# An attention, routing and feed-forward kernel: GpSimd takes over the splitting of k and q, exponentials go ahead of transposes, and weight splits in the assignment move to VectorE

## The chip, the cores and the metric

The kernel runs on one core of one Trainium2 chip. The metric is the device time of one execution in microseconds; runs are compared by their median. PE is TensorE, DVE is VectorE, ACT is ScalarE, POOL is GpSimd, SP is the engine that issues most transfers.

## The reference

Three parts follow each other, all in float32 on the outside.

```python
# 1. attention within hash buckets; q, k, v: [2, 8, 768, 64], proj: [64, 6]
q_bucket, k_bucket = six sign bits of q @ proj and of k @ proj
scores = where(q_bucket == k_bucket, q @ k.T / 8, -1e9)
attn = exp(scores - rowmax);  attn /= attn.sum() + 1e-9
x = (attn @ v), heads side by side            # [1536, 512]
# 2. eight experts, each takes at most 192 of the 1536 tokens
logits = x @ w_gate                           # [1536, 8]
# greedy: largest logit first; a token goes to one expert, a full expert takes no more
out[tokens of e] = relu(x[tokens of e] @ w1[e]) @ w2[e]      # w1[e]: [512, 1024]
# 3. RMS norm, then a gated feed-forward layer, 512 -> 1536 -> 512
xn = x / sqrt(mean(x*x) + 1e-6) * rms_g
y = (silu(xn @ w_gate2) * (xn @ w_val)) @ w_out
```

The three weights of part 3 arrive as 64-bit floats.

## The kernel before

**Numbers in two parts.** A product that needs float32 precision is done in the matmul type float32r, with each operand split into a rounded high part and the low remainder (`nh`, `nl` for k and q; `wh`, `wl` for the experts' weights). Splitting is two instructions: a rounding copy, and a subtract.

**Attention.** Heads are taken in pairs: 2 batches x 4 pairs, 8 pairs in all. A pair has six tiles of 128 queries, and each of its two heads is one iteration `u`, so 12 iterations for a pair and 96 in all. The program is written out in order by hand (no scheduler); each engine works through its own list. In iteration u stand: six transposes of the probabilities of u into two PSUM tiles and their evacuation (`transp`), the exponential of u+1 (`expo`), the scores of u+2 with their row minimum (`scores`; scores carry a minus sign), half of the product with v (`pv`), and every second iteration the combination of two heads (`comb`, which also multiplies by the experts' gate weights, 64 + 8 columns for a head) and its scaling by the inverse row sums (`rinv`, `comb_v`). PSUM tiles called `m` come from a pool of three that transposes, combination and preparation share.

**Work filled in between.** A table `fill` adds work to iterations: the preparation of the next pair and the conversion of the 64-bit weights. Preparation `prep_t` transposes half of k or q (three transposes), ACT writes the rounded `nh` from PSUM, DVE subtracts into `nl`; 4 halves for a pair, 28 in all, since the first pair is prepared by other code. `prep_d` sends `nh` and `nl` into stacked operands by transfers on SP. `prep_p` (12 products on PE, then one DVE comparison for each half) forms the hash bits; it stands four iterations after the last half of q. Then SP sends the bits (`prep_s`), and one iteration later issues the next pair's loads. A conversion `conv` comes every 2.4 iterations, 36 in all: two DVE instructions, one on ACT, then four on GpSimd one behind the other; its store (`conv_store`) stands on SP four iterations later. SP's list is in order too, so a store that waits holds everything behind it.

**Assignment.** Three rounds of `share` on DVE and PE find who gets which expert: DVE compares whole tables (`above`, into `reach`), PE counts (`reached`), DVE waits for the count. A last step (`choose_left`, `positions`) yields the row numbers; GpSimd gathers rows of x from memory, and all engines take a branch that is for a rare case (`tc.If`). Within the first two rounds stand the splits of the first expert's eight weight pieces (`split_w`): ACT rounds, GpSimd subtracts, and SP loads the next piece into the space that the subtract has released.

**Experts and feed-forward.** These fill the rest of the time, nearly all of it PE work. The change leaves their instructions as they are.

Of the kernel before, what the change touches and what calls it, by code (L numbers as in the profile page):

```python
# [43 lines left out]
def lsh_attention__moe__swiglu_kernel(ctx, tc, q, k, v, proj, m_wg, m_w1, m_w2,  # L44
# [158 lines left out]
    def split_w(i, dve_hi, pool_lo):  # L203
        raw = WR.pop(i)
        WH[i] = wth.tile([128, 1024], F32R, name="wh")
        WL[i] = wth.tile([128, 1024], F32R, name="wl")
        if dve_hi:
            nc.vector.tensor_copy(WH[i], raw)
        else:
            nc.scalar.activation(WH[i], raw, AF.Copy)  # L210
        (nc.gpsimd if pool_lo else nc.vector).tensor_tensor(WL[i], raw, WH[i], op=OP.subtract)  # L211
        if i + 8 < 8 * E:
            load_w(i + 8)

# [19 lines left out]
    def conv(n):  # L234
# [9 lines left out]
        nc.gpsimd.tensor_scalar(ha.bitcast(F32), ha.bitcast(F32), MINEXP, None, op0=OP.max)  # L244
# [9 lines left out]
    NAT, STK = {}, {}  # L254

    def prep_t(p, nm, half):
        if half == 0:
            NAT[nm, p] = (nat.tile([128, S], F32R, name="nh_" + nm),
                          nat.tile([128, S], F32R, name="nl_" + nm))
            if nm == "k":  # L260
                SG[p] = nat.tile([128, S], F32R, name="sg")
# [3 lines left out]
        for i in range(TPB // 2):  # L265
            nc.tensor.transpose(t[:, i * 128:(i + 1) * 128],
                                LD[nm, p][:, half * (TPB // 2) + i].rearrange("p h d -> p (h d)"), ident)
        if nm == "q":
            nc.scalar.activation(nh[:, cs], t[:, :HALF], AF.Copy, scale=QS)
            nc.vector.scalar_tensor_tensor(nl[:, cs], t[:, :HALF], QS, nh[:, cs], op0=OP.mult, op1=OP.subtract)  # L270
        else:
            nc.scalar.activation(nh[:, cs], t[:, :HALF], AF.Copy)
            nc.vector.tensor_tensor(nl[:, cs], t[:, :HALF], nh[:, cs], op=OP.subtract)
# [36 lines left out]
    def scores(u):  # L310
# [12 lines left out]
        for n in range(2):  # L323
# [4 lines left out]
        nc.vector.scalar_tensor_tensor(rs[:, h, 2:3], rs[:, h, 0:1], BIG / 2, rs[:, h, 0:1],  # L328
                                       op0=OP.is_lt, op1=OP.mult)
# [10 lines left out]
    def transp(u):  # L340
        pt = PR.pop(u).rearrange("p a b -> p (a b)")
        o = wk.tile([128, TPB, 128], F32, name="pt", bufs=4)
        for half in range(2):
# [4 lines left out]
            if half == 0 or u % 4 < ACT_EVAC:  # L348
                nc.scalar.activation(o[:, 3 * half:3 * half + 3, :], t, AF.Copy)  # L349
            else:  # L350
                nc.vector.tensor_copy(o[:, 3:6, :], t)
# [34 lines left out]
    def rinv(i):  # L386
        rs = RS.pop(i)
        ri = wk.tile([128, 2, 2], F32, name="ri", bufs=2)
        nc.vector.tensor_scalar(ri[:, :, 0], rs[:, :, 3], 1e-9, None, op0=OP.add)
# [3 lines left out]
    def comb_v(i):  # L393
# [292 lines left out]

    def share(r, pieces=()):
        t1 = aw.tile(SH, F32, name="t1")
# [17 lines left out]
        for i in pieces:  # L706
            split_w(i, False, True)
# [9 lines left out]
        above(1, 1)  # L717
        pf = reached(1)
# [545 lines left out]
```

## Time and profile before

| | us |
|---|---|
| three timed runs | 843.48, 842.15, 839.46; median 842.15 |
| profiled execution, its own time | 836.1 |
| its span, first to last instruction | 834.3 |
| PE / DVE / ACT / POOL busy in the span | 763.9 / 553.6 / 398.9 / 329.7 |

The span is what the trace covers; 1.8 us of the profiled execution lie around it. Busy time is an average over stages with different limits: attention runs to about 303 us, the assignment to about 354, experts and feed-forward to the end.

### The profile page before, as it was taken

How to read it: one execution, taken by the hardware profiler on the slowest of the kernel's cores; microseconds unless marked ns; L12 is line 12 of the kernel's file. 1: busy time of each engine (PE TensorE's matmuls, PEld its weight loads, DVE VectorE, ACT ScalarE, POOL GpSimd, SP SyncE). 2: the span in 40 equal slices, each digit the busy share in tenths (PEclk: the TensorE clock that was granted, in tenths of full speed). 3: DMA queues.
4: the chain of work that ended last, by engine and by line, in shares of the span. 5: the costliest groups of instructions: out<-in, count | busy, mean ns of one | idle time of the engine just before them, and what ended most of it. 6: DMA issues, size and time to landing. Idle time of an engine off the chain costs nothing.

```text
span 834.3 us, 14721 instructions
## 1 busy us (share of the span) xinstructions
PE 763.9 (92%) x5317; PEld 685.0 (82%) x5317; DVE 553.6 (66%) x1345; ACT 398.9 (48%) x863; POOL 329.7 (40%) x251
## 2 busy tenths in 40 slices
PE   7999999998999952499999998999999999999996
PEld 4787777777878842289989998999999999999996
DVE  7799899899999987558888776575432332233222
ACT  3676667676676770057767765544311221121111
POOL 3077777766777856237657662000100010001001
PEclk7999999999999995599999999999999999999999
DMA  3678879796988425137767833274200010001000
GB/s 77 170 205 243 229 234 287 210 298 189 265 216 239 156 69 165 28 95 246 228 200 228 265 119 114 76 228 126 80 23 1 30 47 0 1 1 39 1 1 38
DMA packets 95474, 114.00 MB, mean 137 GB/s; under 512 B 31404, under 2 KB 68268, under 8 KB 95396
## 3 DMA queue, kind: packets, MB, share of 16 engines
q1 hardware_dynamic: 93316, 106.71, 43.6%
q0 software_dynamic: 1920, 6.29, 2.1%
q8 instruction: 44, 0.72, 0.4%
q14 instruction: 34, 0.28, 0.1%
q10 hardware_dynamic: 160, 0.00, 0.0%
HBM read 76.83 MB, written 18.09 MB: 114 GB/s over the span
## 4 chain that ended last, share of the span: by engine, by line
PE 35%; issue 18%; DVE 2%; POOL 1%; ACT 1%; DMA 1%; SPq 0%; POOLq 0%; ACTq 0%; DVEq 0%
PE pg L1151 6%; PE pv L1151 6%; PE py L994 6%; PE po L1179 6%; PE ph L970 4%; PE py L996 3%; PE ph L972 2%; POOL out_dram L1187 1%; PE ph L948 1%; DMA fraw<-wv_d 1%; DVE wl L211 0%; PE py L1067 0%; PE px L1026 0%; DVE yn L1056 0%; DVE xl L930 0%
## 5 line engine op out<-in xcount | busy, mean ns | idle before, releaser
L1187 POOL DMA_INDIRECT out_dram<-ot,oi x12 | 11.7, 975 | 312.3 <-DVE ot L1185 310.5
L211 POOL TENSOR_TENSOR wl<-wr,wh 128x1024 fp32r<-128x1024 f32 x43 | 106.3, 2485 | 52.8 <-PE ph L948 20.3
L336 ACT ACTIVATE pr<-sc,rs 128x768 f32<-128x768 f32 x96 | 95.2, 992 | 20.2 <-DVE rs L328 16.0
L347 PE MATMUL m<-ident,pr 128*128 128x128 f32 x576 | 85.6, 282 | 13.2 <-ACT pr L336 8.3
L1160 DVE TENSOR_TENSOR a<-sg,pg 128x384 f32<-128x384 f32 x48 | 26.6, 553 | 105.6 <-ACT sg L1158 105.6
L326 DVE TENSOR_REDUCE rs<-sc 128x1 f32<-128x768 f32 x96 | 91.1, 949 | 7.9 <-PE sc L324 6.2
L244 POOL TENSOR_SCALAR ha<-ha 128x512 f32<-128x512 f32 x36 | 57.3, 1593 | 90.7 <-DVE ha L242 90.7
L347 PEld LDWEIGHTS m<-ident,pr 128*128 128x128 f32 x576 | 62.1, 140 | 30.8 <-ACT pr L336 16.3
L366 PE MATMUL xo<-pt,ld_v 128*64 128x128 f32 x1128 | 82.3, 281 | 0.0
L970 PE MATMUL ph<-xg,wh 128*128 128x384 f32 x256 | 75.3, 362 | 6.5 <-DVE ht L987 5.8
L349 ACT ACTIVATE pt<-m 128x384 f32<-128x384 f32 x120 | 56.3, 490 | 51.2 <-PE m L347 50.5
L994 PE MATMUL py<-ht,wh 128*128 128x384 f32 x256 | 77.3, 366 | 0.0
L1158 ACT ACTIVATE sg<-pg 128x384 f32<-128x384 f32 x48 | 23.5, 490 | 108.7 <-PE pg L1151 108.7
L366 PEld LDWEIGHTS xo<-pt,ld_v 128*64 128x64 f32 x1128 | 59.6, 136 | 18.6 <-issue 11.7
L1164 ACT ACTIVATE ah<-a 128x384 fp32r<-128x384 f32 x48 | 25.2, 525 | 99.8 <-DVE a L1161 99.8
L1151 PE MATMUL pg<-xh,gl 128*128 128x384 f32 x192 | 64.6, 336 | 0.0
L1151 PE MATMUL pg<-xl,gh 128*128 128x384 f32 x192 | 64.5, 336 | 0.0
L1151 PE MATMUL pg<-xh,gh 128*128 128x384 f32 x192 | 64.5, 336 | 0.0
L1151 PE MATMUL pv<-xh,vl 128*128 128x384 f32 x192 | 64.4, 335 | 0.0
L1151 PE MATMUL pv<-xl,vh 128*128 128x384 f32 x192 | 64.4, 335 | 0.0
L1151 PE MATMUL pv<-xh,vh 128*128 128x384 f32 x192 | 64.4, 335 | 0.0
L996 PE MATMUL py<-ht,wl 128*128 128x192 f32 x256 | 64.0, 254 | 0.0
(249 smaller groups left out, 1976.9 us busy)
## 6 DMA issues: line engine op xcount, KB each, us to landing
wr<-in_moe_w_dram SPq DMA_DIRECT2D x64, 512.0 KB
w<-in_moe_w_gate_dram SPq DMA_DIRECT2D x12, 512.0 KB
w<-in_moe_w_val_dram SPq DMA_DIRECT2D x12, 512.0 KB
w<-in_moe_w_out_dram SPq DMA_DIRECT2D x12, 512.0 KB
s_k<-nh_k SPq DMA_DIRECT2D x28, 192.0 KB
s_q<-nh_q SPq DMA_DIRECT2D x28, 192.0 KB
ld_k<-in_k_dram SPq DMA_DIRECT2D x16, 192.0 KB
ld_q<-in_q_dram SPq DMA_DIRECT2D x16, 192.0 KB
```

Source lines behind the costliest of these rows:

```text
L211: (nc.gpsimd if pool_lo else nc.vector).tensor_tensor(WL[i], raw, WH[i], op=OP.subtract)
L244: nc.gpsimd.tensor_scalar(ha.bitcast(F32), ha.bitcast(F32), MINEXP, None, op0=OP.max)
L326: nc.vector.tensor_reduce(rs[:, h, 0:1], ps[:, :, :HALF], axis=AX.XY, op=OP.min)
L336: nc.scalar.activation(pt, ps[:, :, :HALF], AF.Exp, scale=rs[:, h, 1:2], bias=rs[:, h, 2:3], accum_out=rs[:, h, 3:4])
L347: nc.tensor.transpose(t[:, i, :], pt[:, c * 128:(c + 1) * 128], ident)
L349: nc.scalar.activation(o[:, 3 * half:3 * half + 3, :], t, AF.Copy)
L366: nc.tensor.matmul(xo[64 * h:64 * h + 64], vt[:, h, c, :], a[h][:, c, :], start=(c == 0), stop=(c == TPB - 1))
L970: hi = lambda: nc.tensor.matmul(ph[:, :2 * CAP], wh[:, d], xg[:, d].rearrange("p a b -> p (a b)"), start=(d == 0), stop=(d == KD - 1), ski ...
L994: hi = lambda: nc.tensor.matmul(py[d][:, :2 * CAP], wh[:, ds], ht[:, f].rearrange("p a b -> p (a b)"), start=(f == 0), stop=(f == KF - 1), ...
L996: lo = lambda: nc.tensor.matmul(py[d][:, :CAP], wl[:, ds], ht[:, f, 0], start=False, stop=False, skip_group_check=True)
L1151: nc.tensor.matmul(t[:, :TJ], a[:, d, :], b_[:, d, :], start=(n == 0), stop=(n == 3 * KD - 1))
L1179: nc.tensor.matmul(PO[j][t], a[:, ts], b_, start=(f == 0 and n == 0), stop=(f == KG - 1 and n == 2))
```

## The change

Six edits in attention and one in the assignment. (1) `prep_t`: ACT copies k or q from PSUM to a new tile `raw`, and GpSimd makes `nh` and `nl` from it; DVE has no part in it any more. (2) `expo(u + 1)` stands ahead of `transp(u)`, and of the two evacuations of u the first half goes to DVE and the second to ACT (before, the other way round; one iteration in four has both on ACT). (3) One of the two small instructions behind the row minimum takes a column as pointer operand in place of a second tensor. (4) `rinv` adds 1e-9 column by column. (5) `comb_v` scales all 72 columns of a head at once into a wider `xs`; GpSimd copies the logits' columns to `lp` once for a pair, except for the last pair of a batch, and x is written with one transfer for each head. (6) The first GpSimd instruction of a conversion has two ALU operations, minimum and maximum, instead of one. (7) In the assignment ACT rounds all eight pieces first, DVE does the subtracts: two in each round of `share`, the last two behind the gathers.

```diff
-    def split_w(i, dve_hi, pool_lo):
-        raw = WR.pop(i)
+    def split_hi(i, dve):
         WH[i] = wth.tile([128, 1024], F32R, name="wh")
         WL[i] = wth.tile([128, 1024], F32R, name="wl")
...
+    def split_lo(i, pool):
+        (nc.gpsimd if pool else nc.vector).tensor_tensor(WL[i], WR.pop(i), WH[i], op=OP.subtract)
         if i + 8 < 8 * E:
             load_w(i + 8)
+
+    def split_w(i, dve_hi, pool_lo):
+        split_hi(i, dve_hi)
+        split_lo(i, pool_lo)
...
-        nc.gpsimd.tensor_scalar(ha.bitcast(F32), ha.bitcast(F32), MINEXP, None, op0=OP.max)
+        nc.gpsimd.tensor_scalar(ha.bitcast(F32), ha.bitcast(F32), 3.0e38, MINEXP, op0=OP.min, op1=OP.max)
...
+            RAW[nm, p] = nat.tile([128, S], F32, name="nr_" + nm)
...
         if nm == "q":
-            nc.scalar.activation(nh[:, cs], t[:, :HALF], AF.Copy, scale=QS)
-            nc.vector.scalar_tensor_tensor(nl[:, cs], t[:, :HALF], QS, nh[:, cs], op0=OP.mult, op1=OP.subtract)
+            nc.scalar.activation(raw[:, cs], t[:, :HALF], AF.Copy, scale=QS)
         else:
-            nc.scalar.activation(nh[:, cs], t[:, :HALF], AF.Copy)
-            nc.vector.tensor_tensor(nl[:, cs], t[:, :HALF], nh[:, cs], op=OP.subtract)
+            nc.scalar.activation(raw[:, cs], t[:, :HALF], AF.Copy)
+        nc.gpsimd.tensor_copy(nh[:, cs], raw[:, cs])
+        nc.gpsimd.tensor_tensor(nl[:, cs], raw[:, cs], nh[:, cs], op=OP.subtract)
...
-        nc.vector.scalar_tensor_tensor(rs[:, h, 2:3], rs[:, h, 0:1], BIG / 2, rs[:, h, 0:1],
-                                       op0=OP.is_lt, op1=OP.mult)
+        nc.vector.tensor_scalar(rs[:, h, 2:3], rs[:, h, 0:1], BIG / 2, rs[:, h, 0:1], op0=OP.is_lt, op1=OP.mult)
...
-            if half == 0 or u % 4 < ACT_EVAC:
+            if half == 1 or u % 4 < ACT_EVAC:
                 nc.scalar.activation(o[:, 3 * half:3 * half + 3, :], t, AF.Copy)
             else:
-                nc.vector.tensor_copy(o[:, 3:6, :], t)
+                nc.vector.tensor_copy(o[:, 0:3, :], t)
...
-        nc.vector.tensor_scalar(ri[:, :, 0], rs[:, :, 3], 1e-9, None, op0=OP.add)
+        for h in range(2):
+            nc.vector.tensor_scalar(ri[:, h, 0:1], rs[:, h, 3:4], 1e-9, None, op0=OP.add)
...
-            XS[p] = wk.tile([128, TPB, 2, D], F32, name="xs", bufs=2)
+            XS[p] = wk.tile([128, TPB, 2, W], F32, name="xs", bufs=2)
...
+        if hp == HP - 1:
+            nc.vector.tensor_tensor(lp[:, c, 2 * hp:2 * hp + 2, :], pcv[:, :, D:],
+                                    ri[:, :, 1:2].to_broadcast([128, 2, E]), op=OP.mult)
         if i < NU // 2 - 1:
-            nc.vector.tensor_tensor(XS[p][:, t], pcv[:, :, :D],
-                                    ri[:, :, 1:2].to_broadcast([128, 2, D]), op=OP.mult)
+            nc.vector.tensor_tensor(XS[p][:, t], pcv, ri[:, :, 1:2].to_broadcast([128, 2, W]), op=OP.mult)
+        if t == TPB - 1 and hp < HP - 1:
+            nc.gpsimd.tensor_copy(lp[:, b * TPB:(b + 1) * TPB, 2 * hp:2 * hp + 2, :], XS[p][:, :, :, D:])
...
     for u in range(NU + 3):
+
+        if u + 1 < NU:
+            expo(u + 1)
         if u < NU:
             transp(u)
-        if u + 1 < NU:
-            expo(u + 1)
...
     def share(r, pieces=()):
...
-        for i in pieces:
-            split_w(i, False, True)
+        piece()
         pn = reached(0)
...
         above(1, 1)
+        piece()
         pf = reached(1)
...
+    for i in range(8):
+        split_hi(i, False)
     for r in range(3):
-        share(r, (range(0, 4), range(4, 8), ())[r])
+        share(r, range(2 * r, 2 * r + 2))
...
+    for i in (6, 7):
+        split_lo(i, False)
     rv = flagged()
```

`piece()` takes the next number of `pieces` and calls `split_lo` for it on DVE.

The order of the instructions shows the moves at three places. The first is ACT in the first iterations of attention. Before, an evacuation of transposes (`pt`) stands ahead of each exponential (`pr`):

```order
L349 ACTIVATE pt_868<-m_869 128x384
L336 ACTIVATE pr_879,rs_822<-sc_823,rs_822 128x768
L371 ACTIVATE xt_898<-xo_835 128x128
L269 ACTIVATE nh_q_900<-m_902 128x384
L349 ACTIVATE pt_909<-m_910 128x384
L336 ACTIVATE pr_920,rs_822<-sc_881,rs_822 128x768
```

And in the changed kernel, at the same place:

```order
L342 ACTIVATE pr_877,rs_831<-sc_832,rs_831 128x768
L355 ACTIVATE pt_879<-m_885 128x384
L377 ACTIVATE xt_908<-xo_843 128x128
L276 ACTIVATE nr_q_912<-m_913 128x384
L342 ACTIVATE pr_921,rs_831<-sc_890,rs_831 128x768
L355 ACTIVATE pt_923<-m_929 128x384
```

The exponential has changed places with the evacuation of the iteration before it, and ACT writes `nr_q` (raw) where it wrote `nh_q`.

The second place is GpSimd in the middle of attention. Before, its list there holds nothing but conversions, four instructions each:

```order
L244 TENSOR_SCALAR ha<-ha 128x512
L245 TENSOR_TENSOR ha<-ha,eight 128x512
L246 TENSOR_TENSOR ha<-ha,lr 128x512
L247 TENSOR_TENSOR ha<-ha,sg 128x512
L244 TENSOR_SCALAR ha<-ha 128x512
```

And now, around the second half of a preparation (`nr` is raw):

```order
L249 TENSOR_SCALAR ha<-ha 128x512
L250 TENSOR_TENSOR ha<-ha,eight 128x512
L251 TENSOR_TENSOR ha<-ha,lr 128x512
L252 TENSOR_TENSOR ha<-ha,sg 128x512
L279 CAST nh_q<-nr_q 128x384
L280 TENSOR_TENSOR nl_q<-nr_q,nh_q 128x384
L414 COPY lp<-xs 128x6x16
L249 TENSOR_SCALAR ha<-ha 128x512
```

A rounding and a subtract have come in between two conversions, and once for a pair the copy of the logits' columns.

The third place is DVE in the first round of `share`. Before:

```order
L698 TENSOR_TENSOR oh<-lg,m 128x96
L670 TENSOR_TENSOR reach<-steps,kb 128x1536
L701 TENSOR_REDUCE bids<-oh 128x12
L681 TENSOR_SCALAR full_4541<-prank 128x8
L710 TENSOR_TENSOR t_4545<-oh,pcut 128x96
L712 TENSOR_REDUCE own<-t_4545 128x12
L713 SCALAR_TENSOR_TENSOR kb<-own,kv 128x12
L670 TENSOR_TENSOR reach<-steps,kb 128x1536
L716 TENSOR_SCALAR whole<-pcut 128x8
L670 TENSOR_TENSOR reach<-steps,kb 128x1536
L681 TENSOR_SCALAR full_4579<-prank 128x16
```

And now:

```order
L682 TENSOR_TENSOR reach<-steps,kb 128x1536
L721 TENSOR_REDUCE bids<-oh 128x12
L212 TENSOR_TENSOR wl<-wr,wh 128x1024
L693 TENSOR_SCALAR full_4612<-prank 128x8
L729 TENSOR_TENSOR t_4616<-oh,pcut 128x96
L731 TENSOR_REDUCE own<-t_4616 128x12
L732 SCALAR_TENSOR_TENSOR kb<-own,kv 128x12
L682 TENSOR_TENSOR reach<-steps,kb 128x1536
L735 TENSOR_SCALAR whole<-pcut 128x8
L682 TENSOR_TENSOR reach<-steps,kb 128x1536
L212 TENSOR_TENSOR wl<-wr,wh 128x1024
L693 TENSOR_SCALAR full_4653<-prank 128x16
```

A subtract (`wl`) stands ahead of each of the two instructions (`full`) that wait for PE's count.

## Rows read from the trace of the kernel before

**Rows 1.** Windows, attention: us, busy of PE, PEld, DVE, ACT, POOL, clock, DMA, GB/s.

```profile
22.00:303.00 281.00, 264.68 (x2379) 221.72 (x2378) 253.82 (x682) 192.76 (x423) 187.36 (x144) 1.00 0.78 219
```

**Rows 2.** Timeline of PE: start, duration, line, op, out<-in, [idle before <-releaser].

```profile
22.64 0.82 PE L347 MATMUL m<-ident,pr 128*128 128x128 f32 x6
...
128.96 0.82 PE L347 MATMUL m<-ident,pr 128*128 128x128 f32 x6
...
131.84 0.83 PE L347 MATMUL m<-ident,pr 128*128 128x128 f32 x6
...
146.41 0.88 PE L347 MATMUL m<-ident,pr 128*128 128x128 f32 x6 [1.17 <-ACT pr L336]
...
148.97 0.87 PE L347 MATMUL m<-ident,pr 128*128 128x128 f32 x6
...
151.28 0.44 PE L281 MATMUL m<-nh_k,pjt 128*128 128x384 f32 x1
...
153.47 0.82 PE L347 MATMUL m<-ident,pr 128*128 128x128 f32 x6
...
300.29 0.87 PE L347 MATMUL m<-ident,pr 128*128 128x128 f32 x6 [0.17 <-ACT pr L336]
```

**Rows 3.** Waits of PE, 22 to 303 us: us in total, times, longest.

```profile
PE m L347 <- ACT pr L336: 8.3, 15, 1.2
...
PE m L347 <- ACT lr L239: 0.2, 1, 0.2
```

**Rows 4.** Timeline of DVE.

```profile
144.11 1.07 DVE L328 SCALAR_TENSOR_TENSOR rs<-rs 128x1 f32<-128x1 f32 x1
```

**Rows 5.** Groups by line and form, DVE, 22 to 303 us: busy us, mean ns.

```profile
L328 DVE SCALAR_TENSOR_TENSOR rs<-rs 128x1 f32<-128x1 f32 x95 | 30.0, 316 | 0.0
...
L389 DVE TENSOR_SCALAR ri<-rs 128x2 f32<-128x2 f32 x48 | 18.7, 390 | 0.0
...
L327 DVE TENSOR_SCALAR rs<-rs 128x1 f32<-128x1 f32 x95 | 14.6, 154 | 3.3
...
L273 DVE TENSOR_TENSOR nl_k<-m,nh_k 128x384 fp32r<-128x384 f32 x14 | 7.7, 556 | 4.5 <-ACT nh_k L272 4.3
...
L401 DVE TENSOR_TENSOR lp<-m,ri 128x16 f32<-128x16 f32 x46 | 7.6, 165 | 0.0
```

**Rows 6.** Groups by line and form, POOL, same window.

```profile
L244 POOL TENSOR_SCALAR ha<-ha 128x512 f32<-128x512 f32 x36 | 57.3, 1593 | 90.7 <-DVE ha L242 90.7
L247 POOL TENSOR_TENSOR ha<-ha,sg 128x512 int32<-128x512 int32 x36 | 46.1, 1281 | 2.8
...
L245 POOL TENSOR_TENSOR ha<-ha,eight 128x512 int32<-128x512 int32 x36 | 38.1, 1058 | 3.0
```

**Rows 7.** Timeline of POOL in the assignment.

```profile
306.02 20.77 POOL L211 TENSOR_TENSOR wl<-wr,wh 128x1024 fp32r<-128x1024 f32 x8 [0.37 <-ACT wh L210]
```

**Rows 8.** Timeline of DVE in the assignment.

```profile
305.73 0.25 DVE L694 TENSOR_REDUCE kv<-kl 128x12 f32<-128x96 f32 x1
...
334.44 0.26 DVE L654 TENSOR_TENSOR drop<-kl,cut 128x96 f32<-128x96 f32 x1
...
341.83 0.17 DVE L681 TENSOR_SCALAR full<-prank 128x16 bf16<-128x16 f32 x1 [0.98 <-PE prank L678]
...
342.29 0.17 DVE L719 TENSOR_TENSOR cut<-pcut,whole 128x8 f32<-128x8 f32 x1 [0.28 <-PE pcut L684]
```

**Rows 9.** Two lines on DVE: duration ns min/median/max, first and last start us.

```profile
L211 DVE TENSOR_TENSOR wl<-wr,wh x3: 1219/1225/2574, 372.5 to 376.5; 128x1024 fp32r<-128x1024 f32 x3
...
L242 DVE TENSOR_SCALAR ha<-w x36: 406/418/1443, 41.8 to 289.4; 128x512 int32<-128x512 int32 x36
```

**Rows 10.** Timeline of DVE behind the branch.

```profile
353.83 0.17 DVE L887 TENSOR_SCALAR t<-rcs 128x12 f32<-128x12 f32 x1 [4.03 <-DVEq L877]
```

**Rows 11.** Group of splits on POOL, on the page: busy us, mean ns.

```profile
L211 POOL TENSOR_TENSOR wl<-wr,wh 128x1024 fp32r<-128x1024 f32 x43 | 106.3, 2485 | 52.8 <-PE ph L948 20.3
```

**Rows 12.** Timeline of POOL ahead of attention.

```profile
6.92 1.79 POOL L577 COPY cb<-ident 64x64 f32<-64x64 f32 x8
```

More of the change, by code (lines that the diff above doesn't have):

```diff
@@ L201, in load_w @@
         WR[i] = t
-    def split_w(i, dve_hi, pool_lo):
-        raw = WR.pop(i)
+    def split_hi(i, dve):
         WH[i] = wth.tile([128, 1024], F32R, name="wh")
         WL[i] = wth.tile([128, 1024], F32R, name="wl")
-        if dve_hi:
-            nc.vector.tensor_copy(WH[i], raw)
-        else:
-            nc.scalar.activation(WH[i], raw, AF.Copy)
-        (nc.gpsimd if pool_lo else nc.vector).tensor_tensor(WL[i], raw, WH[i], op=OP.subtract)
+        if dve:
+            nc.vector.tensor_copy(WH[i], WR[i])
+        else:
+            nc.scalar.activation(WH[i], WR[i], AF.Copy)
+    def split_lo(i, pool):
+        (nc.gpsimd if pool else nc.vector).tensor_tensor(WL[i], WR.pop(i), WH[i], op=OP.subtract)
         if i + 8 < 8 * E:
             load_w(i + 8)
+    def split_w(i, dve_hi, pool_lo):
+        split_hi(i, dve_hi)
+        split_lo(i, pool_lo)
     convs = []
@@ L252, in conv_store @@
         nc.sync.dma_start(dst[cv_at(src, i)], CV.pop(n).bitcast(F32))
-    NAT, STK = {}, {}
+    NAT, STK, RAW = {}, {}, {}
     def prep_t(p, nm, half):
@@ L267, in prep_t @@
                                 LD[nm, p][:, half * (TPB // 2) + i].rearrange("p h d -> p (h d)"), ident)
+        raw = RAW[nm, p]
         if nm == "q":
-            nc.scalar.activation(nh[:, cs], t[:, :HALF], AF.Copy, scale=QS)
-            nc.vector.scalar_tensor_tensor(nl[:, cs], t[:, :HALF], QS, nh[:, cs], op0=OP.mult, op1=OP.subtract)
-        else:
-            nc.scalar.activation(nh[:, cs], t[:, :HALF], AF.Copy)
-            nc.vector.tensor_tensor(nl[:, cs], t[:, :HALF], nh[:, cs], op=OP.subtract)
+            nc.scalar.activation(raw[:, cs], t[:, :HALF], AF.Copy, scale=QS)
+        else:
+            nc.scalar.activation(raw[:, cs], t[:, :HALF], AF.Copy)
+        nc.gpsimd.tensor_copy(nh[:, cs], raw[:, cs])
+        nc.gpsimd.tensor_tensor(nl[:, cs], raw[:, cs], nh[:, cs], op=OP.subtract)
     def prep_p(p, half):
@@ L410, in comb_v @@
             for h in range(2):
-                nc.scalar.activation(XS[p][:, t, h], pcv[:, h, :D], AF.Copy, scale=ri[:, h, 1:2])
+                nc.scalar.activation(XS[p][:, t, h], pcv[:, h], AF.Copy, scale=ri[:, h, 1:2])
         if t == TPB - 1:
-            nc.sync.dma_start(
-                x_d[b * S:(b + 1) * S, hp * 128:(hp + 1) * 128].rearrange("(c p) d -> p c d", p=128),
-                XS.pop(p).rearrange("p c h d -> p c (h d)"))
+            for h in range(2):
+                nc.sync.dma_start(
+                    x_d[b * S:(b + 1) * S, (2 * hp + h) * D:(2 * hp + h + 1) * D].rearrange("(c p) d -> p c d", p=128),
+                    XS[p][:, :, h, :D])
+            del XS[p]
     def proj_consts():
@@ L687, in share, with piece @@
     def share(r, pieces=()):
+        pieces = iter(pieces)
+        def piece():
+            for i in pieces:
+                split_lo(i, False)
+                break
         t1 = aw.tile(SH, F32, name="t1")
@@ L875, in lsh_attention__moe__swiglu_kernel @@
         gather(0, kk)
+    for i in (6, 7):
+        split_lo(i, False)
     rv = flagged()
```

2 lines of the change are left out of this document (removed).

## The prediction

> **What bounds the kernel now.** I read the stretches first, then TensorE's own order of time, then who it waits for, and last what the two vector engines spend.
>
> The window from 22 to 303 us is the attention stage. In its row [rows 1] no engine is idle for long: PE is busy 264.7 of 281 us, DVE 253.8, ACT 192.8, POOL (GpSimd) 187.4. Busy time does not say which one sets the pace, so the second step is what PE would need if nothing held it. Starts of consecutive blocks tell it [rows 2]: an even iteration u (six transposes, scores, combination, p·v) goes from 146.41 to 148.97, 2.56 us; an odd one from 148.97 to 151.28, 2.31 us; the twelve products of `prep_p` from 151.28 to 153.47, 2.19 us; and an even iteration with three transposes of `prep_t` in it from 128.96 to 131.84, 2.88 us, so those three cost 0.32. From the first transpose of u = 0 (22.64) to that of u = 95 (300.29) there are 48 even and 47 odd iterations: 48 x 2.56 + 47 x 2.31 = 231.4. Seven pairs are prepared on the way: 7 x (4 x 0.32 + 2.19) = 24.3. That makes 255.7 us, and it took 277.65. So **21.9 us** of the stage are PE held up, and no change that leaves PE's work alone can win more there.
>
> What holds it up: the waits of PE in the same window [rows 3]. The largest is for `pr`, the exponential on ACT: 8.3 us in 15 waits. There are eight rows, the first and the last stand here; those that name ACT or DVE add up to 14.0, the one that names a transfer to 1.7. The exponential is late because DVE is: the L328 that gives it scale and bias takes 1.07 us at 144.11 [rows 4], and PE then sits for 1.17 us before 146.41 [rows 2].
>
> Why a one-column instruction takes 1.07 us: the DVE table [rows 5]. L327 is one column from one SBUF operand and takes 0.154 us on average over 95. L328, one column with two SBUF operands, averages 0.316; L389, two columns, 0.390. The excess of the 1.07 us one is about the length of one GpSimd instruction [rows 6], so I read it as DVE waiting for GpSimd in some forms and not in others.
>
> The second place is the assignment. GpSimd runs eight weight splits end to end from 306.02, 20.77 us [rows 7]. Three equal rounds of `share` lie there on DVE: they start at 305.73 and the third ends at 342.29, 36.6 us; but the third, with GpSimd quiet, needs only 334.44 to 342.29, 7.85 us [rows 8].
>
> **The change part by part.**
>
> *Assignment.* No GpSimd split runs in it any more. Three rounds at 7.85 are 23.6 us: 36.6 - 23.6 = **13.0 us** saved. Six of the subtracts move to DVE, at 1.22 us each [rows 9] (fastest of the case, GpSimd not in the way). Each stands where DVE would wait for PE to count, 0.98 us before 341.83 [rows 8]; the other gap of a round is somewhat shorter. Bounds: six times 1.22 - 0.98, that is 1.4, and 7.3 with no cover. I take 2.0, since the cover is there in every round. The last two subtracts come after the gathers and ahead of the branch. Behind them on DVE stand the branch and `t3`, and for DVE's arrival PE waits. DVE today waits 4.03 us there before 353.83 [rows 10], so the two are either inside that time (0) or ahead of it (2.4). The two weight loads that they release also fall beside the gathers. I take 1.2. ACT's eight roundings ran as one run before and still do. Net: 13.0 - 2.0 - 1.2 = **9.8 us**.
>
> *Attention, DVE.* It loses 14 + 14 subtracts `nl` at 0.556 (15 us), 48 small L401 (7.6, less some for the wider joint product: 7), the waits in L328 and L389. New L328 has one tensor operand and a one-column pointer; bounds 0.154 (L327) and 0.316 (as now); I take 0.2, which is nearest to L327's form: 11 us less. L389 becomes two one-column instructions; these follow each other faster than they last, 4 us less as a floor. Together 37 of 253.8. Against it: L242 waits too (median 0.418, longest 1.443 [rows 9]) and keeps its form; it will meet a busier GpSimd, and were it to wait half a 1.3 us instruction every time, that is 36 x 0.65 = 23 us at most. DVE goes to 217 to 240 us, under PE's 256.
>
> *Attention, ACT.* exp(u+1) now stands ahead of the evacuation of u. Before, the exponential queued behind an evacuation that waits for PE, which waited for the exponential before it; that ring is cut. Work is the same: `raw` costs what `nh` did, one evacuation changes halves.
>
> *Attention, GpSimd.* This is the term that can spoil the rest. Its 187.4 us get 28 roundings and 28 subtracts of 384 columns, and six `lp` copies. Subtract: 384/1024 of 2.485 [rows 11] is 0.93. Rounding: no row has it; a copy of 64 columns takes 1.79/8 = 0.22 [rows 12], so between 0.22 and six times that, 1.34; I take 0.75, midway. With starts 0.08 apart from ends, 28 x (0.93 + 0.75 + 0.16) = 51, `lp` 2. L244 changes too: one ALU operation becomes two. Bounds: 0.22 (the copy) and twice its 1.593, 3.19. It reads one tensor of 512 and yet takes longer than L245 (1.058, one tensor and one column) and L247 (1.281, two tensors) [rows 6], so its time is no price of reading; I take L245's 1.06, the row with the same operands. GpSimd: 187.4 - 36 x 0.53 + 51 + 2 = 221 us, 240 if L244 stays as it is. Its first conversion cannot start before 42, so if PE's waits vanish there are 281 - 20 - 20 = 241 us for it. It fits, at nine tenths busy. What queues behind it: `prep_p` on PE (four iterations, about 10 us, after the last half), the stack transfers on SP, and behind them on SP the next pair's loads, for which PE waits 1.7 us already.
>
> The Trainium skill, "GPSIMD Engine Reference", section 4.1 (Engine selection), says against this move that elementwise work belongs on VectorE, GpSimd being about 2x slower for two inputs. By that page a subtract would be 2 x 0.556 = 1.1 (estimate), 5 us more in all. The row gives 0.93, so the trace is milder, and I keep it.
>
> *The rest.* x is written in 16 transfers instead of 8, in runs of 64 floats; the last is issued as attention ends and read by the gathers a whole assignment later; that distance hides it, and without it one more transfer's issue would show. Nothing behind the branch changes.
>
> Of PE's 14.0 us of waits for ACT and DVE I count **13** as won; the transfer wait and the stretches between waits stay. Sum: 836.1 (the profiled execution, whose span is 834.3) - 13 - 9.8 = 813.3. The three timed runs have a median of 842.15, 6.05 above the profiled one; I forecast for the median: 842.15 - 22.8 = **819 us**.
>
> **The rivals.**
>
> A. GpSimd takes over as the bound of attention. For it: 240 us of work in 241 if the new L244 gains nothing, and 256 if the rounding costs 1.34 as well. Then conversions lag, SP stands behind their stores, the next pair's loads come late and PE waits there. Against it: the results of conversions are needed only in the kernel's last stage, so a late one alone holds nobody. Attention wins 0 to 7, the assignment its 9.8: 825 to 832 us.
>
> B. Slower. One mechanism: two ALU operations in L244 cost two passes. GpSimd's list after 42 is then 179 + 36 t us, against 261 until 303. The gain of 9.8 is used up at t = 2.5 us; at t = 3.19 attention ends 33 us later, and the time is 842 + 33 - 10 = 865. Against it: L245's operands at 1.06.
>
> C. GpSimd's one-tensor instructions are cheap, near the copy row's end: L244 0.5, rounding 0.4. Then GpSimd has 190 us of work, never holds anybody, and attention comes close to PE's sum: 20 of the 21.9. Time: 842 - 20 - 10 = 812. The trace speaks against it with L244's 1.593 for one operation and for it with the copy row. The Trainium skill, the same section 4.1, holds that one-input work on GpSimd runs at roughly line rate, which is this case; L244 as it stands disagrees.
>
> D. The new rs form still waits for GpSimd: DVE keeps 11 us, still below PE; the forecast moves by 3 to 5 us and stays in its range.
>
> **How the numbers follow.** Forecast with D 0.58 (814 to 825), A 0.20, C 0.13, B 0.07, anything else 0.02. The range runs from C's end, with the full 21.9 and the assignment at 12 (808), to A's far end plus 3 us of unequal runs (835). A difference of 0.5%, 4.2 us, is about what a measurement of this kernel can tell. Faster by more than that: forecast, A and C, less the part of A that could vanish, 0.89; within 0.04; slower 0.07.
>
> **What the changed profile would show.** Right: DVE L328's and L389's successors at 0.15 to 0.2 throughout; waits of PE for `pr` under 3 us; a gap from the first transpose to that of u = 95 near 265 us; three rounds of `share` of about 8.5 us each; GpSimd 215 to 225 us busy in attention with L244's successor near 1.1. Wrong, by A: GpSimd without idle time and PE waiting for `nl` or for `ld_k`; by B: L244's successor over 2.5 us; for the assignment: PE's restart after the branch more than 3 us later than the last `gi`, measured against today's.

## The result and the profile after

The changed kernel takes 827.03 us (median of 828.43, 823.67, 831.96 and 825.64) against 840.81 for the kernel before on the same chip: ratio 0.987, 95% interval 0.9832 to 0.9908. By the medians it is faster by 13.8 us, where 22.8 were forecast; the ratio, which the interval belongs to, is not the quotient of the two medians (0.984) and puts the gain at 11 us (8 to 14). The profiled execution took 828.43 us, with a span of 826.3.

Attention's row in the windows of the changed kernel, 22 to 303 us, columns as in [rows 1]:

```profile
22.00:303.00 281.00, 265.54 (x2384) 223.58 (x2382) 228.85 (x676) 191.50 (x427) 199.38 (x208) 0.99 0.80 219
```

Over the whole span PE is busy 766.7 us, DVE 524.7, ACT 396.5 and POOL (GpSimd) 320.9. In attention DVE lost 25 us of work and POOL gained 12, no more. Yet PE's timeline of the changed kernel, from the transposes of u = 0 to those of u = 95, with a held-up place between them, and the restart behind the branch at its end:

```profile
22.63 0.82 PE L353 MATMUL m<-ident,pr 128*128 128x128 f32 x6
...
120.99 0.88 PE L353 MATMUL m<-ident,pr 128*128 128x128 f32 x6 [0.48 <-ACT pr L342]
...
124.40 0.58 PE L331 MATMUL sc<-s_k,s_q 82*128 82x384 f32 x2 [2.18 <-issue]
...
297.56 0.88 PE L353 MATMUL m<-ident,pr 128*128 128x128 f32 x6
...
338.76 2.29 PE L1091 MATMUL py<-ones_b 128*128 128x512 bf16 x5 [2.65 <-DVEq L901]
...
343.45 0.66 PE L972 MATMUL ph<-ident,xrow 128*128 128x128 f32 x4 [1.39 <-DMA xrow<-x_d,gi]
...
345.09 0.66 PE L994 MATMUL ph<-xg,wh 128*128 128x384 f32 x1 [0.55 <-issue]
```

The stretch is 297.56 - 22.63 = 274.93 us, against 277.65 in [rows 2]: attention won 2.7 us where 13 were forecast. The new hole is at L331, the product of the scores that reads the sign bits (s2 stacks): first iteration of a pair, 2.18 us. (The trace names no releaser for it here; in the pair that starts near 266 us it names the transfer of the sign bits, `s_q<-sg`, for the same instruction.) PE's waits in the changed kernel, 22 to 303 us, have it on top, and the wait for `pr` in [rows 3] is down from 8.3 to 3.0:

```profile
PE sc L331 <- issue: 4.4, 2, 2.2
PE m L353 <- ACT pr L342: 3.0, 5, 1.3
PE m L353 <- ACT pt L355: 2.1, 5, 0.4
```

The groups of DVE and of POOL in the changed kernel, same stretch, against [rows 5, 6]:

```profile
L247 DVE TENSOR_SCALAR ha<-w 128x512 int32<-128x512 int32 x36 | 26.6, 739 | 10.6 <-DMA wg_d<-ha 4.6 <-DMA wv_d<-ha 4.1 <-DMA wo_d<-ha 1.9
L335 DVE TENSOR_SCALAR rs<-rs 128x1 f32<-128x1 f32 x95 | 19.4, 204 | 0.0
L396 DVE TENSOR_SCALAR ri<-rs 128x1 f32<-128x1 f32 x96 | 9.8, 144 | 0.0
...
L249 POOL TENSOR_SCALAR ha<-ha 128x512 f32<-128x512 f32 x36 | 24.8, 689 | 32.2 <-DVE ha L247 32.2
L280 POOL TENSOR_TENSOR nl_q<-nr_q,nh_q 128x384 fp32r<-128x384 f32 x14 | 14.5, 1035 | 1.1
L279 POOL CAST nh_q<-nr_q 128x384 fp32r<-128x384 f32 x14 | 8.3, 591 | 9.5 <-ACT nr_q L276 9.5
L279 POOL CAST nh_k<-nr_k 128x384 fp32r<-128x384 f32 x14 | 7.2, 516 | 31.9 <-ACT nr_k L278 31.1 <-DMA ld_v<-in_v_dram 0.7
```

L249 went from 1593 to 689 ns by being given a second operation. DVE's L247 went from 588 on average to 739, and DVE now stands 10.6 us for the conversions' stores in front of it.

The assignment, on DVE in the changed kernel (the first instruction of round one, the last of round three, the last two subtracts, `t3` behind the branch):

```profile
303.00 0.25 DVE L714 TENSOR_REDUCE kv<-kl 128x12 f32<-128x96 f32 x1
...
325.69 1.22 DVE L212 TENSOR_TENSOR wl<-wr,wh 128x1024 fp32r<-128x1024 f32 x1
327.28 0.17 DVE L739 TENSOR_TENSOR cut<-pcut,whole 128x8 f32<-128x8 f32 x1 [0.29 <-PE pcut L696]
...
334.71 2.35 DVE L212 TENSOR_TENSOR wl<-wr,wh 128x1024 fp32r<-128x1024 f32 x2
338.82 0.17 DVE L911 TENSOR_SCALAR t<-rcs 128x12 f32<-128x12 f32 x1 [1.76 <-DVEq L901]
```

Three rounds take 327.28 - 303.00 = 24.3 us instead of 36.6 [rows 8]. In front of `t3`, 2.35 us of subtracts and 1.76 of waiting stand where 4.03 of waiting stood [rows 10].

From u = 95 to the first product of layer one it is now 345.09 - 297.56 = 47.5 us; before, that product started at 358.77, 58.5 us behind u = 95. So layer one starts 13.7 us earlier; but the span ends only 8.0 earlier. On the way 1.6 us are lost in the first block of layer one (10.84 us until layer two, 9.27 before) and 3.8 in its fifth, where the change alters no instruction. In the fifth PE waits 3.13 us for DVE instead of 0.87, and from 437.2 to 441.0 its granted clock is 0.55, near the lower of its two levels (1.2 GHz), where the same block ran at 1.00 before. There DVE and POOL each start a subtract of a weight piece at the same moment. DVE's and POOL's timelines in the kernel before:

```profile
441.94 1.21 DVE L211 TENSOR_TENSOR wl<-wr,wh 128x1024 fp32r<-128x1024 f32 x1
...
441.94 3.46 POOL L211 TENSOR_TENSOR wl<-wr,wh 128x1024 fp32r<-128x1024 f32 x1 [0.33 <-ACT wh L210]
```

In the changed kernel, with PE behind it:

```profile
429.88 3.44 DVE L212 TENSOR_TENSOR wl<-wr,wh 128x1024 fp32r<-128x1024 f32 x1
...
429.86 2.39 POOL L212 TENSOR_TENSOR wl<-wr,wh 128x1024 fp32r<-128x1024 f32 x1 [0.32 <-ACT wh L209]
...
435.71 0.44 PE L994 MATMUL ph<-xg,wh 128*128 128x384 f32 x1 [3.13 <-DVE ht L1011]
```

One of the two goes at its own speed (1.21 or 2.39 us), the other takes that on top. The Trainium skill, "SBUF — State Buffer", section "Who interferes with whom", has it that a DVE instruction with two SBUF inputs contends with a GpSimd instruction that reads SBUF, and that issue order decides who blocks; that the first to issue holds the shared pair for its whole instruction it says of another case, DVE's two-port modes. The trace shows such blocking here: 3.46 is 1.21 plus 2.25, 3.44 is 2.39 plus 1.05. Who wins goes with a few hundredths of a us: in the 14 kernels of this case POOL's recorded lead is 0.02 to 0.04 us in the seven where DVE loses (the changed kernel, a1_assign, a4_split, d_slots, d_noload, e_cols, g_slots_order), and at most 0.02 in the others. So the ends of two spans can't be compared to within 4 us; single stretches can. Whether a kernel loses in all its runs no trace shows, so a median may carry these us too; the changed kernel, a4_split and d_slots, on which the argument rests, are all among the seven.

### The profile page after: what moved, and what is told of

The parts are those of the page before. It is cut to its first block, busy times and chain, and to the rows that moved or that the text cites. A ratio compares the mean times of both kernels' runs of the same rounds, so it can differ in the third digit from the quotient of the medians.

```text
span 826.3 us, 14742 instructions
## 1 busy us (share of the span) xinstructions
PE 766.7 (93%) x5317; PEld 689.9 (83%) x5317; DVE 524.7 (64%) x1337; ACT 396.5 (48%) x863; POOL 320.9 (39%) x305
## 4 chain that ended last, share of the span: by engine, by line
PE 35%; issue 19%; DVE 2%; DMA 1%; POOL 1%; ACT 1%; SPq 0%; POOLq 0%; another core or an unknown queue 0%; ACTq 0%; DVEq 0%
PE pg L1175 6%; PE pv L1175 6%; PE py L1018 6%; PE po L1203 6%; PE ph L994 5%; PE py L1020 3%; PE ph L996 2%; POOL out_dram L1211 1%; DMA xrow<-x_d,gi 1%; PE ph L972 1%; DMA fraw<-wo_d 1%; DVE wl L212 0%; PE px L1050 0%; DVE yn L1080 0%; DVE xl L954 0%
## 5 line engine op out<-in xcount | busy, mean ns | idle before, releaser
L212 POOL TENSOR_TENSOR wl<-wr,wh 128x1024 fp32r<-128x1024 f32 x35 | 84.7, 2428 | 59.3 <-PE ph L972 20.4
L333 DVE TENSOR_REDUCE rs<-sc 128x1 f32<-128x768 f32 x96 | 91.4, 952 | 24.3 <-PE sc L331 24.0
L994 PE MATMUL ph<-xg,wh 128*128 128x384 f32 x256 | 78.2, 373 | 8.9 <-DVE ht L1011 8.0
L328 PE MATMUL sc<-s_k,s_q 128*128 128x384 f32 x192 | 57.9, 383 | 0.0
```

The costliest lines, as they stand in the source:

```text
L212: (nc.gpsimd if pool else nc.vector).tensor_tensor(WL[i], WR.pop(i), WH[i], op=OP.subtract)
L328: nc.tensor.matmul(ps[:, n, :HALF], q1[:, h, qs], k1[:, h, n * HALF:(n + 1) * HALF], start=True, stop=False)
L333: nc.vector.tensor_reduce(rs[:, h, 0:1], ps[:, :, :HALF], axis=AX.XY, op=OP.min)
L994: hi = lambda: nc.tensor.matmul(ph[:, :2 * CAP], wh[:, d], xg[:, d].rearrange("p a b -> p (a b)"), start=(d == 0), stop=(d == KD - 1), ski ...
```

## The experiments

Three theories of where attention's gain went. One: the transfers are full (the DMA engines' share rose from 76.9 to 79.7% of 281 us with the x_d pieces), so stores and sign bits land late. Two: SP, which issues in order, stands for GpSimd's `nh`, and what is queued behind on SP leaves late. Three, added after the first eight runs: GpSimd's new work holds DVE up directly (L247). "Attention" below is the stretch from the transposes of u = 0 to those of u = 95 in the run's profile, as above. The runs are from several chips, on which the kernel before took 835.09 to 840.81 us, so the ratios to it are compared, and not the us: the changed kernel's is 0.987.

**The two parts apart.** a1_assign is the kernel before with only the assignment of the change; a2_attn is the changed kernel with the assignment of before.

```diff
 a1_assign, against before (and the other way round in a2_attn, against after)
+    for i in range(8):
+        split_hi(i, False)
-        share(r, (range(0, 4), range(4, 8), ())[r])
+        share(r, range(2 * r, 2 * r + 2))
...
+    for i in (6, 7):
+        split_lo(i, False)
```

> The kernel before with the assignment part alone of the change. The trace of after places layer one 13.7 us earlier, 2.7 of them from attention, so by it this part is worth about 11 us: 830 against 841 (ratio 0.987), shares 24.3 us instead of 36.6. The rival is that the earlier gathers and weight loads give part of it back behind the branch (slow first matmuls, a late gather): then 833 to 836. The forecast's own term was -9.8 (831).

> The changed kernel with the assignment as before: the attention edits alone. By the profiled runs attention ends 2.7 us earlier, so 836 to 839 (ratio 0.995 to 0.998). The forecast's term was -13, 828 (0.985). If the medians' difference of 13.8 is the sum of both parts and the assignment is worth 11, this one gives about 3.

Measured: a1_assign 827.19 us, ratio 0.9884 (0.9853 to 0.9915), attention 279.26; a2_attn 836.88, ratio 0.9984 (0.996 to 1.0007), attention 275.40. The parts add up: 1.16% and 0.16% against 1.3% for both. The assignment is the whole gain; the six edits in attention together are no difference that can be told. Nor is a us or two of attention's stretch in one profile: a1_assign has the attention of before, and 279.26 us of it against 277.65.

**The edits of attention, undone one at a time.**

```diff
 a3_xd: comb_v as before (x and logits scaled apart, one x_d transfer for a pair)
-            nc.vector.tensor_tensor(XS[p][:, t], pcv, ri[:, :, 1:2].to_broadcast([128, 2, W]), op=OP.mult)
+            nc.vector.tensor_tensor(XS[p][:, t], pcv[:, :, :D],
+                                    ri[:, :, 1:2].to_broadcast([128, 2, D]), op=OP.mult)
 a4_split: prep_t as before (ACT rounds from PSUM, DVE subtracts)
-        nc.gpsimd.tensor_copy(nh[:, cs], raw[:, cs])
-        nc.gpsimd.tensor_tensor(nl[:, cs], raw[:, cs], nh[:, cs], op=OP.subtract)
+            nc.vector.tensor_tensor(nl[:, cs], t[:, :HALF], nh[:, cs], op=OP.subtract)
```

> The changed kernel with x and the logits scaled apart as before, so that each pair's x is stored in one transfer with rows of 512 bytes again. Theory one (the transfers are what is full in attention: the DMA engines' share rose from 76.9 to 79.7 per cent of 281 us, all in the x_d stores): VectorE gets some 6 us of work back, but the share falls to about 77 per cent, VectorE waits less for the conversion's stores (10.6 us now, under 5 expected) and attention ends 2 to 6 us earlier: 821 to 825. Theory two (SP's order behind GpSimd): nothing in the stalls changes, and the time is the same or 1 us worse, 827 to 829.

> The changed kernel with k and q split from PSUM by ScalarE and VectorE as before; all other edits stay. Theory two (SP stands up to 6.3 us for GpSimd's rounded tiles, 56 us in all, so stores and sign bits leave late): scores no longer wait 2.2 us for s_q at the start of a pair, VectorE's waits for stores fall below 5 us, attention ends 4 to 8 us earlier: 819 to 823. Theory one (transfers full): the stalls stay where they are, VectorE has 16 us more work, and the time is 827 to 832.

Measured: a3_xd 824.48 us, 0.9871 (0.9834 to 0.9907), attention 271.63, share of the DMA engines 78.0%, DVE's waits for stores 10.1 us, as before it. a4_split 820.07 us, 0.9784 (0.9754 to 0.9813), attention 270.66, no wait of PE for sign bits, waits for stores 4.3. With the x_d pieces undone the ratio stays, though this profile's attention is 3.3 us shorter, and PE still waits 4.1 us for sign bits; so they are not the main cause. The split on GpSimd is: by the ratios it costs 7 us, where the forecast counted it as relief for DVE.

```diff
 b_max
-        nc.gpsimd.tensor_scalar(ha.bitcast(F32), ha.bitcast(F32), 3.0e38, MINEXP, op0=OP.min, op1=OP.max)
+        nc.gpsimd.tensor_scalar(ha.bitcast(F32), ha.bitcast(F32), MINEXP, None, op0=OP.max)
 b_ha6
-        ha = cv.tile([128, 512], I32, name="ha", bufs=3)
+        ha = cv.tile([128, 512], I32, name="ha", bufs=6)
 b_order: transp(u) ahead of expo(u + 1) again
```

> The changed kernel with the conversion's first GpSimd instruction back to one operation (max alone, 1593 ns by rows 6, against 689 ns in the trace of after): 36 times 0.9 us more on GpSimd, 199 us busy becomes about 232 of 281. Theory two (what is late on GpSimd makes SP stand, and with it stores, sign bits and loads): SP's waits for GpSimd's tiles grow from 56 us by some 10 to 20, scores wait longer for s_q, and the time is 831 to 838. Theory one (transfers full) and the view that GpSimd is far from full: 826 to 829.

> The changed kernel with six buffers instead of three for ha, the tile that the conversion stores. VectorE no longer waits for stores (10.6 us in after, 0 expected). If that wait is how SP's delay reaches the time, attention ends 4 to 8 us earlier: 819 to 823, as with the split undone. If the late sign bits (scores waiting 2.2 us for s_q, twice) are it, those stay and the time is 825 to 828.

> The changed kernel with the transposes of u ahead of exp(u+1) again. By the forecast the new order is what takes the exponential's lateness away (8.3 us in 15 waits of PE for it before): without it 4 to 8 us slower, 831 to 835. By the rival, that those waits only changed their place (the evacuations of the transposes now stand behind the exponential), no difference: 826 to 829.

b_max: 844.61 us, 1.011 (1.0073 to 1.0147), slower than the kernel before by 1% and than the changed one by 2.4%, 20 us. Windows of b_max from the first conversion to the end of its attention (316.97 - 22.63 = 294.34), and its L249 (window from 22 to 297 us, with 34 of the 36):

```profile
42.00:317.00 275.00, 251.54 (x2190) 210.93 (x2188) 220.51 (x622) 176.23 (x393) 226.00 (x199) 0.96 0.78 212
...
L249 POOL TENSOR_SCALAR ha<-ha 128x512 f32<-128x512 f32 x34 | 52.5, 1544 | 20.1 <-DVE ha L247 20.1
```

GpSimd is busy 226 of 275 us, not full, and the stage is 19 us longer all the same: SP's waits for `nh` grew from 56 to 73 us (38.6 and 34.6), DVE's for stores from 10.6 to 20.1, those of PE for `pr` from 3.0 to 10.6. Nearly half of the 19 us are not waits: in attention PE is busy 270.3 us with the 2339 instructions that take 261.6 in the changed kernel, at a granted clock of 0.96 instead of 0.99, with stretches at 0.50, the lower level (130 to 134, 206 to 210 and 246 to 250 us), each within 4 us behind a wait of PE of 1.1 to 2.1 us. So GpSimd need not be full for its lateness to cost; whether it came by way of SP or of the stores that DVE waits for was not separated here.

b_ha6: 823.06 us, 0.9839 (0.9818 to 0.9859), between the two expectations in us; by its ratio it is 827 of 840.81, inside the second. DVE's waits for stores are gone, but attention is 276.23 us, no shorter, and PE's waits for sign bits grew to 5.7 + 1.1: the stores were not the way by which the delay came, the sign bits are. b_order: 826.73 us, 0.9889 (0.9868 to 0.9911), attention 278.32, PE's waits for `pr` 5.9: not to be told from the changed kernel, but the intervals are too wide to exclude 4 us, the low end of what the forecast's view expected.

**What is late, and why.** GpSimd's timeline in the changed kernel, around the second half of q of pair 3, counted from 0, the third that is prepared here (ACT wrote that half's `nr_q` from 103.51 to 104.00):

```profile
101.95 0.71 POOL L279 CAST nh_q<-nr_q 128x384 fp32r<-128x384 f32 x1
102.74 1.10 POOL L280 TENSOR_TENSOR nl_q<-nr_q,nh_q 128x384 fp32r<-128x384 f32 x1
103.78 0.26 POOL L414 COPY lp<-xs 128x96 f32<-128x96 f32 x1
104.01 0.62 POOL L249 TENSOR_SCALAR ha<-ha 128x512 f32<-128x512 f32 x1
104.71 1.04 POOL L250 TENSOR_TENSOR ha<-ha,eight 128x512 int32<-128x512 int32 x1
105.83 1.27 POOL L251 TENSOR_TENSOR ha<-ha,lr 128x512 int32<-128x512 int32 x1
107.18 1.28 POOL L252 TENSOR_TENSOR ha<-ha,sg 128x512 int32<-128x512 int32 x1
108.41 0.50 POOL L279 CAST nh_q<-nr_q 128x384 fp32r<-128x384 f32 x1
```

The half is there at 104.00, and a whole conversion, that stands one place ahead in GpSimd's order, keeps it until 108.41. In the pairs after the first prepared one it is the same, 4.1 to 4.5 us. SP's issues in the changed kernel, the first transfer of the q stacks, the last store ahead of the sign bits, and the sign bits of the same pair:

```profile
108.94 0.47 SPq L303 DMA_DIRECT2D s_q<-nh_q  x1
...
116.29 0.51 SPq L257 DMA_DIRECT2D wg_d<-ha  x1
116.89 1.59 SPq L313 DMA_DIRECT2D s_k<-sg  x2
118.52 1.44 SPq L313 DMA_DIRECT2D s_q<-sg  x2
```

Before, that first transfer left at 105.92, in a4_split at 105.43. d_slots leaves everything on GpSimd and changes a number, the iteration of q's second half:

```diff
-SLOTS = (-1, 0, 1, 3, 7, 7)
+SLOTS = (-1, 0, 1, 2, 7, 7)
```

> The changed kernel with the second half of q transposed one iteration earlier (the fourth entry of SLOTS 2 instead of 3), for pairs two to seven. Theory two (the six transfers of the q stacks leave 3.5 us later than with the split undone, at 108.94 instead of 105.43 us in the third pair, and the stores and sign bits behind them are late): SP gets there one iteration, 2.5 us, earlier, scores wait under 2 us in all for sign bits, and the time is 821 to 824. Theory three (what the split costs is VectorE held up by GpSimd's instructions beside it: its first conversion instruction takes 739 ns instead of 478): unchanged, 825 to 829.

d_noload tests the transfers by taking load off them; c_split_xd is a3_xd and a4_split together, and e_cols takes the single columns off it.

```diff
 d_noload: loads only for n < 3, CV[n] is tile n % 3
-        nc.sync.dma_start(w, src[cv_at(src, i)])
+        if n < 3:
+            nc.sync.dma_start(w, src[cv_at(src, i)])
 e_cols
-        nc.vector.tensor_scalar(rs[:, h, 2:3], rs[:, h, 0:1], BIG / 2, rs[:, h, 0:1], op0=OP.is_lt, op1=OP.mult)
+        nc.vector.scalar_tensor_tensor(rs[:, h, 2:3], rs[:, h, 0:1], BIG / 2, rs[:, h, 0:1],
+                                       op0=OP.is_lt, op1=OP.mult)
-            nc.vector.tensor_scalar(ri[:, h, 0:1], rs[:, h, 3:4], 1e-9, None, op0=OP.add)
+        nc.vector.tensor_scalar(ri[:, :, 0], rs[:, :, 3], 1e-9, None, op0=OP.add)
```

> The changed kernel with 33 of the 36 loads of the conversion left out (512 KB each, 17.3 of the 61.7 MB that move in attention): the conversions work on the first three tiles again and again, so the gate, value and output weights are wrong. Theory one (transfers full): the share of the DMA engines falls from 80 to about 58 per cent, all waits for stores and sign bits go, and attention ends 6 to 10 us earlier: 817 to 821. Theories two and three (SP behind GpSimd, VectorE held up): the transfers land sooner, but SP's 56 us of waits for GpSimd's tiles and VectorE's 739 ns stay, and the time is 823 to 828.

> The changed kernel with both the split of k and q and the scaling of x and logits as before; the order, the min and max, the single columns and the assignment stay. If the joint scaling is worth its 6 us on VectorE, this is 2 to 5 us slower than with the split alone undone: 822 to 826. If its 256 byte packets cost as much on the transfers, the same 818 to 822.

> The kernel with the split and the scaling as before (measured at 0.982), and the row sums in their old forms too: the third column of rs from two scalars of one instruction, the reciprocal's sum over both heads at once. By rows 5 these are 0.11 us more on VectorE 95 times and some 0.1 us more 48 times, with waits of up to 1.07 us behind them, 15 us in all: if VectorE's work is what delays the exponential, 825 to 829. If it lies beside PE's work, 818 to 822.

d_slots: 819.18 us, 0.9789 (0.975 to 0.9827), as good as undoing the split. GpSimd's timeline at the same place in d_slots:

```profile
101.81 0.70 POOL L279 CAST nh_q<-nr_q 128x384 fp32r<-128x384 f32 x1
102.59 1.06 POOL L280 TENSOR_TENSOR nl_q<-nr_q,nh_q 128x384 fp32r<-128x384 f32 x1
103.60 0.26 POOL L414 COPY lp<-xs 128x96 f32<-128x96 f32 x1
103.80 0.50 POOL L279 CAST nh_q<-nr_q 128x384 fp32r<-128x384 f32 x1
104.39 1.00 POOL L280 TENSOR_TENSOR nl_q<-nr_q,nh_q 128x384 fp32r<-128x384 f32 x1
105.36 0.61 POOL L249 TENSOR_SCALAR ha<-ha 128x512 f32<-128x512 f32 x1
```

Both halves now stand ahead of the conversion. SP's issues at the same places, and PE's last block, in d_slots:

```profile
104.33 0.47 SPq L303 DMA_DIRECT2D s_q<-nh_q  x1
...
111.79 0.73 SPq L257 DMA_DIRECT2D wg_d<-ha  x1
116.38 1.60 SPq L313 DMA_DIRECT2D s_k<-sg  x2
118.04 1.44 SPq L313 DMA_DIRECT2D s_q<-sg  x2
...
288.75 0.87 PE L353 MATMUL m<-ident,pr 128*128 128x128 f32 x6
```

Attention is 288.75 - 22.63 = 266.12 us, 8.8 less than in the changed kernel: PE's waits for sign bits (4.8), for `pr` (2.6 less) and for `pt` (1.5 less) make that up. SP's waits in the changed kernel, 22 to 303 us:

```profile
SPq L303 <- POOL nh_k L279: 30.1, 6, 6.3
SPq L303 <- POOL nh_q L279: 25.7, 7, 5.5
```

And in d_slots:

```profile
SPq L303 <- POOL nh_k L279: 24.8, 6, 6.3
SPq L303 <- POOL nh_q L279: 8.1, 6, 5.6
```

PE waits nowhere for sign bits. These do not leave late in either kernel: DVE has them ready at 116.52 in the changed kernel and at 116.36 in d_slots, and SP issues them 0.4 and 0.02 us later. It is their landing that is late, with PE's product held to 124.40 where it ran at 121.35 in d_slots. In the changed kernel SP, behind since the stack transfers, issues without a pause from 108.94 on, two loads of 512 KB and a store close ahead of the sign bits, and from 119 to 121 us 319 GB/s move; in d_slots the same transfers left by 112.5, SP then waited for the bits, and 90 GB/s move. Nor does SP stand longer in all: its waits from 22 to 303 us sum to 151 us before, 127 in the changed kernel and 136 in d_slots.

L247 still takes 677 ns on average, and between 78 and 258 us the DMA engines' share is 0.91, as in the changed kernel. So theory three falls (with 677 ns instead of a4_split's 478 d_slots is as fast, so what holds DVE up costs nothing that shows), and theory one alone falls too.

d_noload: 817.18 us, 0.9768 (0.9731 to 0.9806), attention 266.65. SP's waits for `nh` stay (36.5 and 36.7 us), the share falls from 0.80 to 0.62, and PE's waits for sign bits fall from 4.8 to 1.3. So either cure does it: the sign bits land late where the transfers ahead of them left late and are still under way. Theories one and two are halves of one mechanism.

c_split_xd: 819.92 us, 0.9817 (0.9792 to 0.9841), attention 269.91; e_cols: 824.6 us, 0.9867 (0.9829 to 0.9904), attention 273.41. The columns are worth 3.5 us in the profiles (PE's waits for `pr` are 4.2 without them, 0.9 with them); the two intervals overlap, so this is likely and not settled. Likewise the joint scaling: 0.9784 with it and 0.9817 without, overlapping.

**The order once more**, where nothing else is late (d_slots with transp(u) ahead of expo(u + 1)):

```diff
 g_slots_order, against d_slots
-        if u + 1 < NU:
-            expo(u + 1)
         if u < NU:
             transp(u)
+        if u + 1 < NU:
+            expo(u + 1)
```

> The changed kernel with q's second half one iteration earlier (measured at 0.979) and, against that, the transposes of u ahead of exp(u+1) again. In the changed kernel itself the order made no difference that could be told (0.989 against 0.987), but there the late sign bits covered it. If the order takes the exponential's lateness off PE as forecast, this is 4 to 8 us slower than with the new order: 823 to 827 (0.984 to 0.989), and PE waits for pr again. If it only moves the waits, 817 to 821 (0.976 to 0.982).

820.76 us, 0.9773 (0.9735 to 0.9811), attention 267.17, against 0.9789 and 266.12: no difference, and here the two intervals leave no room for the 4 to 8 us. PE's largest waits in g_slots_order, 22 to 290 us:

```profile
PE m L353 <- ACT nr_q L276: 1.9, 8, 0.3
PE m L353 <- ACT pr L342: 1.5, 4, 0.5
```

The 8.3 us of [rows 3] are down to 1.5 in the old order as well.

The versions with the fourth slot at 2, or with the split undone, beat both kernels: 0.979 and 0.978 against 0.987 (the intervals end at 0.9827 and 0.9813, below 0.9832).

## Why the prediction was right in sign and too large

The time lies inside the stated range, but outside the forecast's own 814 to 825 and inside rival A's 825 to 832, without GpSimd as the bound; that the sign is right is owed to the assignment, not to attention.

- **Assignment, 9.8 forecast: right.** a1_assign is worth 1.16% of 837.43, 9.7 us. The terms were off both ways: 24.3 us for three rounds instead of 23.6 + 2.0 (six subtracts cost 0.7, not 2.0), the last two subtracts nothing instead of 1.2 (inside DVE's wait at the branch). "Nothing behind the branch changes" was wrong: the second gather lands 1.39 us after PE asks for it, and layer one starts 6.33 us behind the restart instead of 5.00. That it is the weight loads, released earlier, that hold the gather up was not tried. By the stretch from u = 95 to layer one the part is worth 58.5 - 47.5 = 11.0; the errors have opposite signs, so that the sum came so close is partly luck.
- **Attention, 13 forecast: 1.3 us (a2_attn).** DVE was freed as forecast (228.9 us busy, inside 217 to 240) and the waits for `pr` fell to 3.0. The step that failed stands in the part on GpSimd: "It fits, at nine tenths busy." It gives no price to what queues behind GpSimd: it names `prep_p`, the stack transfers and the next loads and stops there, because GpSimd has time left. GpSimd had even more time left than that, 199.4 busy for 221, and still a half of q waited 4.4 us for one conversion, SP with it; the transfers behind left late and close together, and at three pairs PE waited for the sign bits to land. d_slots, which has all the work on the same engines and only changes a place in the order, gets 8.8 of the missing us back; from before it is 277.65 - 266.12 = 11.5 of the forecast 13.
- **Sizes on GpSimd.** L249 0.69 us (taken 1.06, bounds 0.22 to 3.19), rounding 0.52 to 0.59 (taken 0.75), subtract 1.0 (taken 0.93). With them GpSimd's 199.4 us are nearer to rival C's 190 than to the forecast's 221, but C's time (812) did not come: it too counted only busy time, and even d_slots, without the delay, wins 11.5 of its 20 in attention. The Trainium skill, "GPSIMD Engine Reference", section 4.1 (Engine selection), has one-input work roughly at line rate; L249 now comes nearer to that, with 0.69 us against the 0.42 of DVE's one-input instruction on a tile of the same size (L243 in the kernel before), and max alone, at 1.59, does not.
- **Rival A** was the mechanism in half: SP stood behind GpSimd and PE behind SP, without GpSimd being the bound. With L244's old form the cost was more than its 825 to 832 (b_max, 844.61), and GpSimd was not full even then (226.0 of 275 us).
- **Rival B** (two operations, two passes) fell: the second operation made the instruction faster. **D** fell: L335 0.204, as taken, L396 0.144.
- **The cut ring on ACT.** The forecast put the exponential's lateness down to ACT's order as well as to DVE. The order made no difference to the time that can be told, twice (b_order, g_slots_order); in g_slots_order the waits for `pr` are 1.5 us in the old order, in b_order 5.9 against 3.0. Which of the other edits brought them down was not taken apart; e_cols (4.2) and b_max (10.6) show that the columns and the second operation of L249 have a part in it.
- **DVE's L242** did meet the busier GpSimd, 151 ns more on average, 5.4 us in all, within the 23 allowed; d_slots, as fast as a4_split with 677 ns against 478, shows nothing that it costs.

## What to carry to other kernels

An engine that works in order can be late without being full. When work moves to one, write down what stands ahead of the moved instruction in that engine's order and how long that takes, and follow who is in line behind its result, the queue that issues transfers above all, and what it then sends close together; a sum of busy times finds none of it. Before a move is given up for its cost, try to place it one slot earlier: here one number was worth as much as undoing it.

## What the runs showed of the hardware

- GpSimd's tensor_scalar on 128x512 f32 takes 1593 ns with max alone and 689 ns with min and max (1544 again in b_max, and the time rises by 20 us, so the duration in the trace is real).
- Two-tensor subtracts of 128x1024 that start within 40 ns of each other on DVE and GpSimd: one runs at its own speed (DVE 1.21, GpSimd 2.39), the other takes 3.44 to 3.47. In the changed kernel, where the loser is DVE, the block of PE that waits for it is 3.8 us longer.
- The first block of layer one took 9.3 to 12.2 us over the runs, with the same products. In the changed kernel (10.8) the granted clock is 0.51 from 345.0 to 348.4, about the lower level, and the first product takes 0.66 us; before (9.3) it is 1.00 from the start and 0.41. What decides it was not tested.
- Some waits of PE are followed by a lower clock. In the changed kernel the wait of 2.19 us that ends at 231.45 is followed by a granted clock of 0.80 and 0.77 (230 to 238 us); that of 2.18 us at 124.40 is not followed by a fall.
